# Two quarter-loads of gate weights change queues at the start of a fused layernorm, SSM and SwiGLU kernel

## The chip, the cores and the metric

The kernel runs on 1 core of one Trainium2 chip. The time is the device time of one execution in microseconds (us). Before the change it is 179.15 us (median of 3 runs, 179.12 to 179.2). Times inside an execution are counted from the start of the profiled span, which is about 1.7 us shorter than the device time. PE is TensorE, ACT is ScalarE, DVE is VectorE, SP is SyncE. The mean granted TensorE clock is 1.0 unless said.

## The reference, cut to what matters

```python
xn = _layernorm(x, axis=-1)                    # x: 2048 x 512, bf16
return x + _A_ref(xn, ...) + _B_ref(xn, ...)   # A: a diagonal SSM, B: SwiGLU

def _B_ref(x, w_gate, w_up, w_down):           # w_gate: 512 x 1376
    g = _silu(x @ w_gate)
    u = x @ w_up
    return (g * u) @ w_down
```

The gate product contracts over 512 rows of `w_gate`. The kernel holds them as four K tiles (0 to 3) of 128 rows. A gate output is four matmuls, one for each K tile, accumulated in PSUM. The loads discussed here bring the first 896 of the 1376 columns of `w_gate` (7 output tiles of 128); a later load brings the rest.

## The kernel before

The kernel records tasks with their dependences. It then orders ACT's, DVE's and Pool's tasks with a list scheduler of its own that works on estimated times. PE's and SP's tasks keep the order in which they were recorded. Only the first 13 us concern the change. In them, x tiles 0 to 3 are loaded and normalised while PE runs fillers (warm-up matmuls on constants), and then PE does the first gate matmuls in quarters of 128 tokens. The head of the load order is:

```python
x_load(0)                                    # 128 KB each, on SP's queue
x_load(1)
act_q = [dma("ld_touch", tch[0:16, 0:1], wg_v[0:128:8, 0:1, 0:2], [("tch",)], 16 * 4, eng="act")]
act_q.append(wg_load("a0", 0, 2, eng="act", order=(act_q[-1],)))   # K tiles 0, 1: 448 KB
x_load(2)
act_q.append(wg_load("a1", 2, 3, eng="act", order=(act_q[-1],)))   # K tile 2: 224 KB
wg_load("a2", 3, 4)                                                # K tile 3: 224 KB, on SP's queue
x_load(3)
# ...
act_table(AF.Sqrt, (act_q[-1],))             # small activation: brings the Sqrt table load with it (2.22 to 3.51 us)
```

DVE works through a fixed chain of statistics. "b" is half a tile's statistics, "s" aggregates them and lets ACT take the square root, "r" is the reciprocal, and "n" normalises half a tile. The half of x tile 2 stands ahead of the reciprocal of tile 1:

```python
for op, a, h in (("r", 0, 0), ("n", 0, 0), ("b", 1, 0), ("b", 1, 1), ("s", 1, 0), ("b", 2, 0),
                 ("r", 1, 0), ("n", 1, 0), ("n", 1, 1), ...
```

PE uses the K tiles one after the other for the first quarter: 7 matmuls (one for each of 7 output tiles) of K tile 0, 7 of K tile 1, 7 of K tile 2, 7 of K tile 3. The first transposes of x tile 1 stand after the fourth matmul of K tile 2:

```python
place = {(0, 2, 4): (1, 0), (1, 0, 2): (1, 1), ...}   # (quarter, first K tile, n): (x tile, half)
for q in range(4):
    for k0, k1 in (((0, 1), (1, 2), (2, 3), (3, 4)), ((0, 1), (1, 2), (2, 4)), ...)[q]:
        for n, (i, bk) in enumerate(tiles):
            if (q, k0, n) in place:
                xt_tile_fine(*place[(q, k0, n)])
            # ... matmuls of K tiles k0 to k1, start=(kt == 0), stop=(kt == KT - 1)
```

So the 1st, 8th, 15th and 22nd gate matmuls are the first users of K tiles 0, 1, 2 and 3.

## Time and profile before

| what | before |
|---|---|
| device time | 179.15 us |
| PE busy, share of the span | 98% |
| K tile 2 landed, first use (15th gate matmul) | 6.17, 6.49 |
| K tile 3 landed, first use (22nd) | 6.76, 7.13 |
| x2 landed | 5.89 |
| first 512-wide gate matmul | 12.93 |

Each of these loads reports in 16 parts, seen in the trace as 16 increments of its semaphore; the "landed" figures are the 16th and last of them. Two lines of the page show what bounds the kernel: busy time of each engine with its share of the span, and the shares of the chain of waits that ended last.

```profile
PE 173.9 (98%) x927; PEld 83.9 (47%) x935; DVE 162.5 (92%) x284; ACT 87.8 (49%) x116; POOL 9.3 (5%) x22
...
PE 98%; issue 0%; DVE 0%
```

PE is almost never idle and the chain runs through PE alone, so a change counts only if it moves a PE instruction. The timeline of the kernel before shows the start. Its columns are start, duration, engine, line, operation, output and inputs, count, and in brackets the engine's idle time before it and what ended that. A "q" after an engine marks its sequencer issuing a DMA.

```profile
0.79 1.34 SPq L402 DMA_DIRECT2D x_sb<-in_A_x_dram  x3
...
1.22 0.97 ACTq L402 DMA_DIRECT2D wg<-in_B_w_gate_dram  x2
...
2.17 0.43 SPq L402 DMA_DIRECT2D wg<-in_B_w_gate_dram  x1
2.22 1.28 ACT L466 ACT_TABLE_LOAD   x1 [2.22 <-issue]
...
3.88 0.29 ACT L524 ACTIVATE sd<-mv,epst 128x1 f32<-128x1 f32 x1
...
5.71 1.17 PE L803 MATMUL pb<-xnT,wg 128*128 128x128 bf16 x18
...
5.92 0.43 DVE L512 BATCH_NORM_STATS2 st<-x_sb 128x6 f32<-128x256 bf16 x1 [0.26 <-DMA x_sb<-in_A_x_dram]
...
6.84 0.29 PE L582 MATMUL pb<-ident,xn_sb 128*128 128x128 bf16 x2
...
12.93 1.03 PE L759 MATMUL pb<-xnT,wg 128*128 128x512 bf16 x4
```

The first 18 gate matmuls run without a break. DVE waits 0.26 us for x2. That puts off the reciprocal of tile 1, and PE stands still for 0.14 us before the transposes at 6.84. The same trace tells how long each weight load took from issue to landing (last column, us); the lines are K tiles 0 and 1, K tile 2 and K tile 3.

```profile
wg<-in_B_w_gate_dram ACTq DMA_DIRECT2D x1, 448.0 KB, 4.0
wg<-in_B_w_gate_dram ACTq DMA_DIRECT2D x1, 224.0 KB, 4.5
wg<-in_B_w_gate_dram SPq DMA_DIRECT2D x1, 224.0 KB, 4.6
```

The two loads of 224 KB take about equally long, but SP's was issued 0.47 us later (2.17 against 1.70) and lands 0.59 us later. The tile on SP's queue is the one that PE uses last.

### The profile page before, as it was taken

The page shows a single profiled execution, that of the slowest core. Times are in us where ns is not written, and L with a number is a line of the kernel's source. Part 1 is how long each engine was busy: PE and PEld are TensorE (multiplying, and loading weights), DVE is VectorE, ACT ScalarE, POOL GpSimd, SP SyncE. Part 2 cuts the span into 40 slices and gives each one's busy share as a digit, 9 for nine tenths or more (in the row PEclk, how much of TensorE's full clock was granted, in tenths as well). Part 3 has the DMA queues.
Part 4 walks back from the last instruction along what each step waited for, and adds up shares of the span by engine and source line. Part 5 has one row for each costly group of instructions (what it writes and reads, how often), then busy time and mean ns, then how long its engine had stood idle before and what let it go on. Part 6 is the DMA issues. An engine that isn't in the chain of part 4 may idle for free.

```text
span 177.5 us, 2421 instructions
## 1 busy us (share of the span) xinstructions
PE 173.9 (98%) x927; PEld 83.9 (47%) x935; DVE 162.5 (92%) x284; ACT 87.8 (49%) x116; POOL 9.3 (5%) x22
## 2 busy tenths in 40 slices
PE   8999999999999999999999999999999999999994
PEld 2894444444444444444444444444444444444743
DVE  2865999899999999999999999999899999999933
ACT  4679979789999665034565560000965520000000
POOL 3022300040000000310000000000000000000000
PEclk9999999999999999999999999999999999999999
DMA  5992694664951000002700000002000000001022
GB/s 155 326 365 67 139 124 96 167 132 101 358 123 24 0 0 0 0 30 69 126 18 0 0 0 4 0 30 76 12 0 4 0 0 0 0 0 53 10 89 89
DMA packets 22966, 12.37 MB, mean 70 GB/s; under 512 B 15180, under 2 KB 22956, under 8 KB 22956
## 3 DMA queue, kind: packets, MB, share of 16 engines
q1 hardware_dynamic: 22508, 11.54, 25.0%
q10 hardware_dynamic: 448, 0.69, 1.2%
q8 instruction: 7, 0.11, 0.3%
q14 instruction: 3, 0.02, 0.0%
HBM read 6.46 MB, written 2.10 MB: 48 GB/s over the span
## 4 chain that ended last, share of the span: by engine, by line
PE 98%; issue 0%; DVE 0%
PE pb L759 36%; PE pb L959 21%; PE pb L876 16%; PE pb L972 15%; PE pb L803 4%; PE pb L477 3%; PE pb L839 2%; PE pb L849 1%; PE pb L582 1%; DVE x_sb L977 0%
## 5 line engine op out<-in xcount | busy, mean ns | idle before, releaser
L916 DVE TENSOR_TENSOR_SCAN rot<-sm,car,rot 128x512 bf16<-128x512 f32 x32 | 39.0, 1266 | 0.1
L959 PE MATMUL pb<-wd,hT 128*128 128x512 bf16 (+3 forms) x194 | 38.1, 355 | 0.2
L759 PE MATMUL pb<-xnT,wu 128*128 128x512 bf16 x160 | 37.3, 380 | 0.0
L759 PE MATMUL pb<-xnT,wg 128*128 128x512 bf16 x132 | 31.3, 380 | 0.0
L972 PE MATMUL pb<-W,hss 128*128 128x512 bf16 (+2 forms) x140 | 28.1, 355 | 0.2
L876 PE MATMUL pb<-xnT,BT 128*128 128x512 bf16 x128 | 28.1, 379 | 0.0
L959 PEld LDWEIGHTS pb<-wd,hT 128*128 128x128 bf16 (+1 forms) x198 | 18.5, 98 | 19.9
L759 PEld LDWEIGHTS pb<-xnT,wu 128*128 128x128 bf16 x160 | 15.6, 98 | 18.9 <-issue 0.2
L771 ACT ACTIVATE sg<-pb 128x1024 bf16<-128x1024 f32 x20 | 20.1, 1024 | 8.6 <-PE pb L759 7.7
L829 ACT ACTIVATE uf<-pb 128x1024 bf16<-128x1024 f32 x20 | 20.5, 1026 | 7.2 <-PE pb L759 5.9
L972 PEld LDWEIGHTS pb<-W,hss 128*128 128x128 bf16 x144 | 13.5, 98 | 14.3
L759 PEld LDWEIGHTS pb<-xnT,wg 128*128 128x128 bf16 x132 | 12.7, 98 | 15.7 <-ACT xn_sb L506 0.4
L876 PEld LDWEIGHTS pb<-xnT,BT 128*128 128x128 bf16 x128 | 12.5, 98 | 15.1
L883 ACT ACTIVATE u_sb<-pb 128x1024 bf16<-128x1024 f32 x16 | 16.2, 1017 | 5.4 <-PE pb L876 5.4
L977 DVE TENSOR_TENSOR x_sb<-pb,x_sb 128x512 bf16<-128x512 f32 (+2 forms) x18 | 11.0, 623 | 3.5 <-PE pb L972 3.5
L831 DVE TENSOR_TENSOR hT<-sg,uf 128x1024 bf16<-128x1024 bf16 x20 | 13.3, 680 | 0.0
L506 ACT ACTIVATE xn_sb<-x_sb,nmr,rstd 128x512 bf16<-128x512 bf16 x8 | 6.0, 804 | 9.2 <-DVE nmr L503 9.2
L858 ACT ACTIVATE sg<-pb 96x1024 bf16<-96x1024 f32 x2 | 2.0, 1013 | 17.1 <-PE pb L839 17.1
L482 DVE BATCH_NORM_STATS2 st<-x_sb 128x6 f32<-128x512 bf16 x12 | 7.4, 681 | 3.1 <-DMA x_sb<-in_A_x_dram 3.1
L907 DVE TENSOR_TENSOR rot<-rot,cosT 128x2048 bf16<-128x2048 bf16 x8 | 9.7, 1215 | 0.1
L907 DVE TENSOR_TENSOR rot<-rot,sin 128x2048 bf16<-128x2048 bf16 x8 | 9.7, 1216 | 0.0
L907 DVE TENSOR_TENSOR rot<-u_sb,cosT 128x2048 bf16<-128x2048 bf16 x8 | 9.7, 1216 | 0.0
(81 smaller groups left out, 144.3 us busy)
## 6 DMA issues: line engine op xcount, KB each, us to landing
out_dram<-x_sb SPq DMA_DIRECT2D x15, 128.0 KB, 1.7
x_sb<-in_A_x_dram SPq DMA_DIRECT2D x3, 512.0 KB, 6.9
wd<-in_B_w_down_dram SPq DMA_DIRECT2D x1, 1280.0 KB, 6.3
wu<-in_B_w_up_dram SPq DMA_DIRECT2D x1, 768.0 KB, 5.5
wu<-in_B_w_up_dram SPq DMA_DIRECT2D x1, 608.0 KB, 7.6
x_sb<-in_A_x_dram SPq DMA_DIRECT2D x4, 128.0 KB, 3.5
wg<-in_B_w_gate_dram SPq DMA_DIRECT2D x1, 480.0 KB, 6.4
wg<-in_B_w_gate_dram ACTq DMA_DIRECT2D x1, 448.0 KB, 4.0
```

Of the source, the lines that this page charges most:

```text
L482: return g.add("dve", lambda e, a=a: e.bn_stats(out=st[:, a, :], in_=x_sb[:, a, :]), reads=[("x", a)], writes=[("st", a)], name="bnst%d" % ...
L759: inst = e.matmul(pbank[0:fs, bk, :].rearrange("p (j t) -> p j t", j=4), lhsT=w[:, kt, i * 128:i * 128 + fs], rhs=xnT[:, c % 2, :, kt, :], ...
L771: g.add("act", lambda e: e.activation(out=sg[rows, sl, 0:n, :].rearrange("p a t -> p (a t)"), in_=pair_f32(rows, bk, 512 * n), func=AF.Sil ...
L829: g.add("act", lambda e: e.activation(out=uf[rows, ul, 0:n, :].rearrange("p a t -> p (a t)"), in_=pair_f32(rows, bk, 512 * n), func=AF.Ide ...
L831: g.add("dve", lambda e: e.tensor_tensor(out=hT[rows, hb, i0:i0 + n, :], in0=sg[rows, sl, 0:n, :], in1=uf[rows, ul, 0:n, :], op=ALU.mult), ...
L876: inst = e.matmul(pbank[:, bk, :].rearrange("p (j t) -> p j t", j=4), lhsT=BT[:, ri, kt, pt * 128:(pt + 1) * 128], rhs=xnT[:, c % 2, :, kt ...
L883: g.add("act", lambda e: e.activation(out=u_sb[:, us].rearrange("p r t -> p (r t)"), in_=pair_f32(slice(0, 128), b0), func=AF.Identity), r ...
L907: tt = lambda out, a, b, op, r, w, nm: g.add("dve", lambda e: e.tensor_tensor(out=out, in0=a, in1=b, op=op), reads=r, writes=w, name="%s_% ...
L916: g.add("dve", lambda e, A0=A0, A1=A1, k=k, ri=ri, pt=pt: e.tensor_tensor_scan(out=A1[:, k, ri, :], data0=rr[:, pt:pt + 1].to_broadcast([1 ...
L959: inst = e.matmul(pbank[:, bk, 0:nc_], lhsT=hT[0:fs, hb, i, lt * 128:(lt + 1) * 128], rhs=wd[0:fs, i, c0:c0 + nc_], start=(i == 0), stop=F ...
L972: inst = e.matmul(pbank[:, bk, 0:nc_], lhsT=hss[:, hb, pt, ri, lt * 128:(lt + 1) * 128], rhs=W12[:, ri, pt, c0:c0 + nc_], start=False, sto ...
L977: g.add("dve", lambda e, bk=bk, a=a, c0=c0, nc_=nc_: e.tensor_tensor(out=x_sb[:, a, c0:c0 + nc_], in0=pbank[:, bk, 0:nc_], in1=x_sb[:, a, ...
```

## The change

Intent, as the diff and its words show it: x2 should meet less traffic. K tile 2 goes to SP's queue behind x2; K tile 3 goes to ACT's queue, behind the Sqrt table load, which can so begin earlier.

```diff
         x_load(2)
-        act_q.append(wg_load("a1", 2, 3, eng="act", order=(act_q[-1],)))
-        wg_load("a2", 3, 4)
+        wg_load("a1", 2, 3)
         x_load(3)
 ...
         act_table(AF.Sqrt, (act_q[-1],))
+        wg_load("a2", 3, 4, eng="act", order=(g.tasks[-1],))
+        hold = {"a2": g.tasks[-1]}
 ...
-        hold = {}
 ...
             reserved.clear()
+            hold["sd0"].od.add(hold["a2"])
```

`order` and `od` are order in the instruction stream, not waits. The last line keeps the first square root behind the issue of K tile 3.

## The prediction

> **What bounds the kernel.** TensorE: 98% busy on the page, and the chain of waits is 98% PE, so only what moves PE matters. The change touches the first 8 us. The timeline there shows fillers (warm-up matmuls) until about 5.0 us, the first gate matmul at 5.71, then 112 gate matmuls 56 ns apart with transposes of x between them. PE pauses there only before transposes: 0.14 us before the first one of x tile 1 (a matmul at 6.65, the transpose at 6.845), 0.03 at 7.67, 0.12 at 9.58. The last two follow ScalarE's evacuations and will recur. The first comes from VectorE: half-tile statistics of x2 stand in its order before the reciprocal of tile 1, and VectorE idled 0.26 us (5.66 to 5.915) for the landing of x2 (5.89).
>
> **Why x2 is late.** Issued at 1.71, its packets run only from 4.25 to 5.44, though x1 before it on SyncE's queue was done at 3.67. ScalarE issued K tile 2 at 1.70, just ahead. My reading: [...] x2's waited until most of K tiles 0 to 2 had drained. [...] from 3.75 to 4.25 ScalarE's moves alone at about 385 KB/us[...].
>
> **What the change does.** K tile 2 (224 KB) goes behind x2 on SyncE (issued about 2.17); K tile 3 goes to ScalarE behind the Sqrt table load and its small activation. The table load starts at about 1.73, not 2.22: worth nothing, as the first square root (3.88) waits for statistics (3.85). I doubt that K tile 3 is really issued after the table load: at 20.91 ScalarE's sequencer is at a wait while four later-executed activations are already queued[...]. I expect the issue at 1.8 to 2.3 (70%), else 3.0 to 3.8. Either leaves the first square root alone within 0.1 us.
>
> Estimates from this trace: x2's packets start about 3.6 and land by 5.2 to 5.5. Then K tiles 2 and 3 share about 385 KB/us (448 KB, 1.2 us): landings 6.2 to 6.6 for K tile 2 (before 6.17, needed at 6.485) and 6.3 to 6.9 for K tile 3 (before 6.76, needed at 7.13).
>
> **On the path.** VectorE's 0.26 us wait goes, the reciprocal of tile 1 comes 0.2 us sooner, PE's 0.14 us gap closes. Everything after is gapless PE, so the shift stays: minus 0.14 us, less some chance that K tile 2 is late (up to plus 0.3). Expected 179.05 us (before 179.15), range 178.75 to 179.4: within 2% 0.985, faster 0.005, slower 0.01.
>
> **What would show it.** Right: no VectorE idle time for x2, first transpose of tile 1 near 6.71, K tile 2's matmuls contiguous, first plain gate matmul (12.93) near 12.79. Wrong: PE pausing near 6.5 or 7.1 for weights; x2 still landing near 5.9[...]; first square root later than 3.9, so that the first gate matmul slips past 5.71.
>
> **What would make it wrong.** K tile 2 landing after 6.5 (it takes the place of the 6.76 landing); the issue on ScalarE blocking the square root; the kernel's static scheduler reordering later ScalarE or VectorE work from changed estimates, some tenths either way.

The sum: 179.15 less the gap of 0.14 is 179.01, and the chance of a late K tile 2 (up to plus 0.3) takes it to 179.05. What the trace itself shows of x2's delay: from 3.75 to 4.25 us ACT's queue moves all but alone, and from 4.25 to 5.25 both queues move. That x2's packets waited for K tiles 0 to 2 was the reading of these times, not shown; the start near 3.6 was an estimate that rests on it.

## The result, and the profile after

The changed kernel takes 179.74 us (median of 6 runs, 179.59 to 180.06), and the kernel before on the same chips 179.14 (6 runs, 178.94 to 179.47). The ratio is 1.0033, 95% interval 1.002 to 1.0046. Ratios here are the mean time of one kernel's fast runs over that of the other's fast runs of the same rounds, so they are not quite the ratio of the quoted medians. The change is within 2% and it is slower, by about 0.6 us, outside the predicted range.

The shares of the chain of waits of the changed kernel:

```profile
PE 94%; DMA 3%; SPq 1%; issue 0%; DVE 0%
```

A DMA is now in the chain. The timeline of the changed kernel (the edit moves most line numbers in this stretch by one):

```profile
0.79 1.34 SPq L402 DMA_DIRECT2D x_sb<-in_A_x_dram  x3
...
1.23 0.45 ACTq L402 DMA_DIRECT2D wg<-in_B_w_gate_dram  x1
...
1.71 1.28 ACT L465 ACT_TABLE_LOAD   x1 [1.71 <-PEq L1076]
1.78 0.42 ACTq L402 DMA_DIRECT2D wg<-in_B_w_gate_dram  x1
...
2.18 0.43 SPq L402 DMA_DIRECT2D wg<-in_B_w_gate_dram  x1
...
3.78 0.29 ACT L523 ACTIVATE sd<-mv,epst 128x1 f32<-128x1 f32 x1 [0.48 <-DVE mv L521]
...
6.01 0.95 PE L802 MATMUL pb<-xnT,wg 128*128 128x128 bf16 x14 [0.33 <-DMA wg<-in_B_w_gate_dram]
...
6.34 0.43 DVE L511 BATCH_NORM_STATS2 st<-x_sb 128x6 f32<-128x256 bf16 x1 [0.48 <-DMA x_sb<-in_A_x_dram]
...
7.38 0.38 PE L802 MATMUL pb<-xnT,wg 128*128 128x128 bf16 x4 [0.41 <-DMA wg<-in_B_w_gate_dram]
...
7.60 0.28 PE L581 MATMUL pb<-ident,xn_sb 128*128 128x128 bf16 x2
...
13.75 0.59 PE L758 MATMUL pb<-xnT,wg 128*128 128x512 bf16 x2
```

The run of 18 matmuls is now 14 and 4. Between them PE waits for `wg`: K tile 2 landed at 7.24, and the 15th matmul starts at 7.38 instead of 6.49. The weight loads of the changed kernel from issue to landing, in the order K tiles 0 and 1, K tile 3, K tile 2:

```profile
wg<-in_B_w_gate_dram ACTq DMA_DIRECT2D x1, 448.0 KB, 4.7
wg<-in_B_w_gate_dram ACTq DMA_DIRECT2D x1, 224.0 KB, 4.9
wg<-in_B_w_gate_dram SPq DMA_DIRECT2D x1, 224.0 KB, 5.1
```

Two more things are to be seen. K tile 3 was issued at 1.78, in the table load and not behind it. And x2 is not earlier but later (6.31). Part of this execution's delay is its own accident: in the trace one of the 16 parts of most loads from x1 on comes 0.4 to 0.7 us behind the other 15 (K tiles 0 and 1: 15 parts by 5.29, the last at 5.96), which also held the first gate matmul to 6.01. One profile cannot say how much of that belongs to the change. The first 15 parts can be compared without this accident: those of K tile 2 were in at 6.77 to 6.82 in all three profiles of the changed kernel, and at 6.10 and 6.15 in the two of the kernel before.

From there on nothing happens to the difference. The first 512-wide gate matmul starts at 13.75 instead of 12.93, and in both executions the device time (180.06 and 179.25) is 166.3 us more than that. The same difference, 166.30 to 166.33, stands in 13 of the 17 profiles, so the start of that matmul tells the time; the four exceptions are named below. The static scheduler did reorder some DVE and ACT work after 14 us, and this constant shows that it costs nothing.

### The profile page after: what moved, and what is told of

It reads as the page before. It is cut to its first block, busy times and chain, and to the rows that moved or that the text cites. A ratio compares the mean times of both kernels' runs of the same rounds, so it can differ in the third digit from the quotient of the medians.

```text
span 178.3 us, 2422 instructions
## 1 busy us (share of the span) xinstructions
PE 173.8 (97%) x927; PEld 83.8 (47%) x935; DVE 163.0 (91%) x284; ACT 88.3 (49%) x116; POOL 9.2 (5%) x22
## 3 DMA queue, kind: packets, MB, share of 16 engines
HBM read 6.46 MB, written 2.10 MB: 48 GB/s over the span
## 4 chain that ended last, share of the span: by engine, by line
PE 94%; DMA 3%; SPq 1%; issue 0%; DVE 0%
PE pb L758 35%; PE pb L959 21%; PE pb L876 15%; PE pb L972 15%; PE pb L802 3%; DMA wg<-in_B_w_gate_dram 3%; PE pb L839 2%; PE pb L849 1%; SPq L402 1%; PE pb L581 1%; DVE x_sb L977 0%
## 5 line engine op out<-in xcount | busy, mean ns | idle before, releaser
L972 PEld LDWEIGHTS pb<-W,hss 128*128 128x128 bf16 x144 | 13.4, 98 | 14.3
L876 PEld LDWEIGHTS pb<-xnT,BT 128*128 128x128 bf16 x128 | 12.5, 98 | 15.1
L907 DVE TENSOR_TENSOR rot<-u_sb,sin 128x2048 bf16<-128x2048 bf16 x8 | 9.7, 1218 | 0.0
```

The source lines that it names most:

```text
L876: inst = e.matmul(pbank[:, bk, :].rearrange("p (j t) -> p j t", j=4), lhsT=BT[:, ri, kt, pt * 128:(pt + 1) * 128], rhs=xnT[:, c % 2, :, kt ...
L907: tt = lambda out, a, b, op, r, w, nm: g.add("dve", lambda e: e.tensor_tensor(out=out, in0=a, in1=b, op=op), reads=r, writes=w, name="%s_% ...
L972: inst = e.matmul(pbank[:, bk, 0:nc_], lhsT=hss[:, hb, pt, ri, lt * 128:(lt + 1) * 128], rhs=W12[:, ri, pt, c0:c0 + nc_], start=False, sto ...
```

## The experiments

Theory T1: the loss is the wait for K tile 2. It took the later place on SP's queue, and PE needs it first. Rival T2: the moved table load, or the order of ACT's instructions, costs the time. Beside these, a question: what holds x2 back, if not what the prediction said?

The kernel before took 179.46 us (median of 9). Kernels are compared only within the same rounds.

### The table load alone

K tile 2 stays on ACT and K tile 3 on SP, as before; the table load goes ahead of ACT's last weight load. Against the changed kernel:

```diff
-        wg_load("a1", 2, 3)
+        wg_load("a2", 3, 4)
 ...
-        wg_load("a2", 3, 4, eng="act", order=(g.tasks[-1],))
+        wg_load("a1", 2, 3, eng="act", order=(g.tasks[-1],))
```

> Edit: the queues keep K tile 2 on ScalarE and K tile 3 on SyncE as before the change; only the Sqrt table load is moved ahead of ScalarE's last weight load. Theory T1 (the loss comes from K tile 2, needed first at about 6.5 us, now being the fifth transfer in SyncE's queue instead of the second on ScalarE's): no loss, 179.0 to 179.3 us, K tile 2 lands 6.1 to 6.4, no pause of the gate matmuls longer than 0.1 us for weights. Rival T2 (the table load or the order of ScalarE's instructions costs the time): 179.6 to 179.8 us, like the change.[...]

Measured: 179.29 us (median of 5), ratio to before 0.9994 (0.9981 to 1.0006). K tile 2 landed at 6.05. The timeline has the unbroken 18 again:

```profile
5.73 1.17 PE L802 MATMUL pb<-xnT,wg 128*128 128x128 bf16 x18
```

T2 is out: with ACT's first 38 us in the order of the changed kernel, apart from which tile its last load carries, no time is lost. (The scheduler's later order of DVE and ACT is here that of the kernel before. It is no rival: the loss arises before 13 us, and the 166.3 us hold with either order.) My reading of the prediction would also have x2 land before 5.5 here, as it is issued ahead of ACT's last load. x2 landed at 5.45, but the bulk of its packets began at 4.2, no earlier than in the kernel before (4.4 and 4.2). That speaks against the reading. ("Bulk" is here and below the ninth of a load's 128 packets.)

### The tiles alone

The table load stays where it was before the change; the two tiles exchange queues. Against before:

```diff
-        act_q.append(wg_load("a1", 2, 3, eng="act", order=(act_q[-1],)))
-        wg_load("a2", 3, 4)
+        act_q.append(wg_load("a2", 3, 4, eng="act", order=(act_q[-1],)))
+        wg_load("a1", 2, 3)
```

> Edit: K tiles 2 and 3 exchange queues, and nothing else; the table load stays behind ScalarE's weight loads as before the change. T1: the whole loss, 179.5 to 179.9 us, with TensorE pausing 0.3 to 0.6 us before the 15th gate matmul for K tile 2. T2: none, 179.0 to 179.3.

Measured: 179.63 us (median of 5), ratio 1.0012 (0.9999 to 1.0024). K tile 2 landed at 6.88, and the wait is back:

```profile
5.74 0.94 PE L803 MATMUL pb<-xnT,wg 128*128 128x128 bf16 x14
...
7.01 0.38 PE L803 MATMUL pb<-xnT,wg 128*128 128x128 bf16 x4 [0.33 <-DMA wg<-in_B_w_gate_dram]
```

This is T1's picture, and DVE's whole order is that of the changed kernel. By time alone the interval just reaches 1; the position of the 15th matmul is what tells.

### The load really behind the table load

The changed kernel, with K tile 3's load waiting on the semaphore of the small activation:

```diff
-        wg_load("a2", 3, 4, eng="act", order=(g.tasks[-1],))
+        wg_load("a2", 3, 4, eng="act", after=(g.tasks[-1],))
```

> Edit: the changed kernel, with K tile 3's load made to wait (semaphore) for the end of the small activation behind the table load, so that it is issued at about 3.35 us, as the change's words say, instead of 1.78. If the early issue of K tile 3 is what lets it run beside K tile 2 and delay it: K tile 2 lands 5.9 to 6.3 and the loss shrinks, to 179.0 to 179.4 us, unless K tile 3 now lands after 7.1 (then a pause there of as much). If K tile 2 is late merely because it is last in SyncE's queue behind x0 to x2: the same as the change, 179.6 to 179.9, K tile 2 near 6.8. T2 gives the same as the change as well, or worse by a later square root.

Measured: 179.92 us (median of 5), ratio 1.0023 (1.001 to 1.0037). The issue moved to 3.33. K tile 2 landed at 6.50 instead of 6.8 to 7.2, so K tile 3 beside it on the other queue is likely part of its delay (one profile). But K tile 3 now landed at 7.38, behind its need at about 7.1, and PE waited for it there (22nd matmul at 7.43). The wait was moved, not removed. (The profile is of the fastest of the five runs, 179.51; what the others lost beyond it was not traced.) x2 landed at 5.99, and its last packet began at 5.29, before K tile 3's first at 5.46. So of ACT's queue only K tiles 0 and 1 moved beside it: the first sign that those two hold it.

### The changed kernel again

> The changed kernel once more, for a second profile. The first shows one of the 16 parts of most landings from x1 on 0.5 to 0.7 us behind the other 15 (K tiles 0 and 1: 5.29, then 5.96), and TensorE waiting for K tiles 0 and 1 as well. If that straggler belongs to the change, it is here again and the first gate matmul starts near 6.0. If it was an accident of that execution, the first gate matmul starts near 5.6 to 5.7, only the pause for K tile 2 is left, and the profiled time is nearer 179.6 than 180.06.

Measured: 179.72 us (median of 5), ratio 1.0019 (1.0005 to 1.0033). The straggler (late last part) of 0.67 us in K tiles 0 and 1 was an accident (here the 15th part came at 5.27 and the last at 5.38; first gate matmul at 5.67). K tile 2 landed at 6.89 and the 15th matmul started at 7.02.

### Both tiles on SyncE

Against before (the kernel before took 179.34 us, median of 11):

```diff
-        act_q.append(wg_load("a1", 2, 3, eng="act", order=(act_q[-1],)))
+        wg_load("a1", 2, 3)
         wg_load("a2", 3, 4)
```

> Edit: before, but K tiles 2 and 3 both on SyncE's queue behind x2, in that order, so that ScalarE carries only K tiles 0 and 1. If K tile 2 was late in the changed kernel because K tile 3 ran beside it on the other queue: K tile 2 now lands 6.2 to 6.5 (packets of it alone after K tiles 0 and 1 are through), no pause over 0.15 us before the 15th gate matmul, K tile 3 lands 6.7 to 6.9, 179.2 to 179.5 us. If it is its place behind x0 to x2 alone: K tile 2 again near 6.8, and the loss is there. x2 starts near 4.25 again, as in all six profiles so far, if K tiles 0 and 1 alone hold it; near 3.6 if a second load on ScalarE held it (my blind reading).

Measured: 179.18 us (median of 6), ratio 0.9992 (0.9977 to 1.0007). K tile 2 landed at 6.13 and K tile 3 at 6.75, both in time. So K tile 2 was in time behind x2 on SP's queue when K tile 3 followed it there instead of running beside it (6.13, against 6.79 to 7.24 in the changed kernel). x2's bulk began at 4.14. The first 512-wide matmul was the earliest of all profiles (12.79), but this execution lost it later: PE waited before 25.25 for the transposed `B_im` (landed 25.20). SP issues that after x4 to x7 have landed (in the kernel before they landed at 15.44, and SP issued `B_re` at 15.52 and `B_im` at 19.66). The extra issue put their load from 6.62 to 7.10. Its landing came at 16.40 (15.44 before, and 14.3 to 16.2 in all 14 profiles in which the issue was not moved), so that the extra issue is the reason is likely, not shown.

### K tiles 0 and 1 behind x2 in order of issue

Against the table-load run, K tiles 0 and 1 move behind the table load on ACT's stream:

```diff
-        act_q.append(wg_load("a0", 0, 2, eng="act", order=(act_q[-1],)))
 ...
+        wg_load("a0", 0, 2, eng="act", order=(g.tasks[-1],))
         wg_load("a1", 2, 3, eng="act", order=(g.tasks[-1],))
```

> Edit: K tile 2 on ScalarE, K tile 3 on SyncE as in the run with the table load alone moved, but K tiles 0 and 1 are issued behind the table load too (about 1.30 instead of 1.23, or, if the table load holds up the issue, after x2's issue at 1.71). If [...] K tiles 0 and 1 hold x2 back: when they are issued after x2, x2's packets start before 3.3 and it lands before 4.8, while K tiles 0 and 1 land 5.3 to 5.8 (needed 5.7). If the issue moves by less than 0.1 us, nothing changes (179.1 to 179.5 us)  and x2's start stays near 4.25: then this run does not tell.

Measured: 187.7 us (median of 6), ratio 1.0469 (1.044 to 1.0498). It does not answer its question: the issue moved only to 1.29, still ahead of x2's at 1.71, and the bulk of x2's packets began at 4.37. The 8 us, which I had not expected, have nothing to do with the queues. With the changed estimates the kernel's own scheduler put the statistics of x4 to x7 between DVE's last two copies of transposed x, and x4 to x7 land after 16 us. Its timeline:

```profile
10.70 0.29 DVE L588 COPY xnT<-pb 128x256 bf16<-128x256 bf16 x1 [0.33 <-PE pb L581]
...
16.25 2.47 DVE L483 BATCH_NORM_STATS2 st<-x_sb 128x6 f32<-128x512 bf16 x4 [5.25 <-DMA x_sb<-in_A_x_dram]
...
18.91 0.26 DVE L588 COPY xnT<-pb 128x256 bf16<-128x256 bf16 x1
...
19.23 1.03 PE L802 MATMUL pb<-xnT,wg 128*128 128x128 bf16 x8 [7.00 <-DVE xnT L588]
```

PE stood still for 7 us, and the granted clock was 0.5 from 15.1 to 21.9 us (mean 0.981). It is the mishap that the prediction named for the changed kernel, at "some tenths" of a us; there it did not happen.

### K tile 3 used first

The changed kernel with its loads untouched, but in the first quarter PE uses K tile 3 before K tile 2:

```diff
-            place = {(0, 2, 4): (1, 0), ...
+            place = {(0, 3, 4): (1, 0), ...
-    for k0, k1 in (((0, 1), (1, 2), (2, 3), (3, 4)), ...
+    for k0, k1 in (((0, 1), (1, 2), (3, 4), (2, 3)), ...
-            start=(kt == 0), stop=(kt == KT - 1))
+            start=(kt == 0), stop=(kt == (2 if q == 0 else KT - 1)))
```

> Edit: the changed kernel, loads untouched, but TensorE uses K tile 3 before K tile 2 for the first x tile (the order in which they land). T1: the pause before the 15th gate matmul shrinks to under 0.15 us (K tile 3 lands 6.2 to 6.3), the 22nd then starts near 7.05 when K tile 2 is in (6.8 to 6.9), 179.2 to 179.5 us. If the loss came from anything else in the change: 179.6 to 179.9 as before.

Measured: 179.64 us (median of 6, 179.09 to 179.72), ratio 1.0009 (0.9991 to 1.0027): it cannot be told from before, and the median lies above what T1 expected. In the profile (179.41 us) the wait for weights is gone; x2 landed at 5.99, so the transposes of x tile 1 came at 6.94.

### The kernel before again

The kernel before, unchanged, for one look.

> The kernel before once more, for a second profile: K tile 2 lands 6.1 to 6.3, the first gate matmul at 5.6 to 5.8 and the first 512-wide one at 12.8 to 13.0; the size of the differences from the first profile is the noise against which landings of single profiles are read.

Measured: 179.43 us in one run (its state is unknown, as for every single run). The expectation was missed: here a straggler hit K tile 2 (15 parts by 6.15, the last at 6.70). The 15th matmul started at 6.83 and the first 512-wide one at 13.13. DVE's statistics of x2 have no wait here (no bracket):

```profile
5.57 0.37 DVE L512 BATCH_NORM_STATS2 st<-x_sb 128x6 f32<-128x256 bf16 x1
...
6.83 0.38 PE L803 MATMUL pb<-xnT,wg 128*128 128x128 bf16 x4 [0.26 <-DMA wg<-in_B_w_gate_dram]
```

So the kernel before can suffer the same wait, in one of its two profiles, by a straggler. The changed kernel waits in all three of its profiles, with one or without. How often stragglers come may be a reason why its ratios range from 1.0019 to 1.0033; the timed runs don't show it.

The kernel before took 179.31 us (median of 11).

### All gate weights on SyncE

```diff
-        act_q.append(wg_load("a0", 0, 2, eng="act", order=(act_q[-1],)))
         x_load(2)
-        act_q.append(wg_load("a1", 2, 3, eng="act", order=(act_q[-1],)))
+        wg_load("a0", 0, 2)
+        wg_load("a1", 2, 3)
         wg_load("a2", 3, 4)
```

> Edit: before, but all gate weights on SyncE's queue behind x2 in the order of need: x0, x1, x2, K tiles 0 and 1, K tile 2, K tile 3, x3; ScalarE carries only a 64-byte load. Question: what holds x2's first packets to about 4.1 to 4.4 us in all ten profiles so far, whatever ScalarE issued after K tiles 0 and 1? If K tiles 0 and 1 on ScalarE's queue do: x2's packets follow x1's without a hole, from 2.6 to 3.2, and x2 lands before 4.5. If x2 is late by itself (third load of the queue): it starts near 4.2 again. K tiles 0 and 1 then land 5.2 to 5.8 (needed 5.7), K tile 2 5.8 to 6.4, so the time is 179.0 to 179.6 us.

Measured: 179.42 us (median of 5), ratio 1.0002 (0.999 to 1.0014). x2's packets began at 2.9 and it landed at 4.06, 1.2 to 2.3 us earlier than in all profiles with K tiles 0 and 1 on ACT's queue (5.26 to 6.31). DVE does not wait for it (nor did it in the second profile of the kernel before; it is the start of the packets that tells). The timeline of this run has no bracket at x2's statistics:

```profile
5.57 0.38 DVE L512 BATCH_NORM_STATS2 st<-x_sb 128x6 f32<-128x256 bf16 x1
```

So K tiles 0 and 1 hold x2 back, not K tile 2. The time is no better: K tiles 0 and 1 now land at 5.70 and hold the first gate matmul to 5.83. And PE lost 0.11 us again near 25 us, where `B_im` landed at 25.06: the matmul at 25.11 starts 0.32 us after the one before it instead of 0.22.

### The changed kernel a third time

> The changed kernel a third time, on the same chip as the next two, as their yardstick: 179.5 to 180.0 us, K tile 2 lands 6.8 to 7.2, the 15th gate matmul about 0.13 us after that.

Measured: 179.71 us (median of 5), ratio 1.0021 (1.0009 to 1.0033). K tile 2 landed at 6.79, the 15th matmul started at 6.92, and the first 512-wide one at 13.29. This execution has no straggler of note (the last parts of x1 to x3 and of the K tiles come at most 0.06 us behind), and PE waits all the same:

```profile
6.92 0.38 PE L802 MATMUL pb<-xnT,wg 128*128 128x128 bf16 x4 [0.27 <-DMA wg<-in_B_w_gate_dram]
```

### K tile 2 one place further back

The changed kernel, with x3 ahead of K tile 2. The instruction order of PE, DVE, ACT and Pool is the same as in the changed kernel:

```diff
-        wg_load("a1", 2, 3)
         x_load(3)
+        wg_load("a1", 2, 3)
```

> Edit: the changed kernel with K tile 2 moved one place further back, behind x3 (128 KB) on SyncE's queue; the instruction order of all other engines is identical. T1, as a matter of dose: K tile 2 lands 0.3 us later than in the changed kernel of this call (7.1 to 7.3), and the time rises by as much, to 0.2 to 0.45 us above the changed kernel. If the landing of K tile 2 is not what costs the time: the same time as the changed kernel within 0.1 us.

Measured: 180.00 us (median of 5, 179.91 to 180.01), ratio to before 1.0035 (1.0023 to 1.0047); that is 0.29 us over the changed kernel (180.00 less 179.71; its runs, 179.61 to 179.83, don't reach these). K tile 2 landed at 7.18, 0.39 us later than there, and the first 512-wide matmul came at 13.69, 0.40 us later:

```profile
7.32 0.38 PE L802 MATMUL pb<-xnT,wg 128*128 128x128 bf16 x4 [0.69 <-DMA wg<-in_B_w_gate_dram]
```

This is the dose that T1 asked for. K tile 2 and x3 change places, nothing else is moved, and the time follows K tile 2's landing: 0.40 us between the two profiled executions (180.01 and 179.61), as between their 512-wide matmuls.

### K tile 3 used first, again

The same kernel as above.

> The changed kernel with TensorE using K tile 3 before K tile 2 for the first x tile, again, because the first measurement (ratio to before 1.0009, interval 0.9991 to 1.0027) could not tell; there the pause had moved to the first transpose of x tile 1, which waited for x2 (landed 5.99). T1: 0.15 to 0.4 us faster than the changed kernel of this call. If the loss is not the wait for K tile 2: no faster.

Measured: 179.60 us (median of 6), ratio to before 1.0007 (0.9991 to 1.0024). The expectation, 0.15 to 0.4 us under the changed kernel, was missed by the median (179.60 against 179.71); the means differ by 0.20 us, but half of the six times lie among or above those of the changed kernel. So time alone does not settle it. The six times fall apart: 179.15, 179.15, 179.47, 179.73, 179.80, 179.88. The profile is of the 179.73 run. Its first 18 gate matmuls are unbroken, but take 1.66 us where others take 1.17:

```profile
5.78 1.66 PE L802 MATMUL pb<-xnT,wg 128*128 128x128 bf16 x18
```

There the first ten start 0.107 us apart, up to 6.74, and from 6.82 on it is 0.056 us: only then did PE come to its full rate ("full clock" below). In the earlier profiles that came between 3.9 and 5.5 us, most often in the fillers. So the moment varies from execution to execution; what sets it is not shown. The delay here is 0.49 us (1.66 less 1.17). By my estimate it would in the changed kernel partly hide in the wait for K tile 2 (0.41 and 0.27 us in its first and third profiles).

The kernel before took 179.46 us (median of 11, 178.89 to 180.04).

### K tile 3 used first, two more profiles

The same kernel, one look each.

> The changed kernel with K tile 3 used before K tile 2, for a profile. So far its times fall in two groups, 179.1 and 179.7. In a profile of 179.73 TensorE's clock came to full only at 6.85 us[...]. T1 with this clock as the reason for the second group: a time under 179.3 has full clock before 5.6 and no pause for weights over 0.2 us; a time over 179.5 has full clock after 6 or another named landing (x2, K tiles 0 and 1) as the reason. If a run over 179.5 has full clock early and no such late landing, T1 lacks something.

> A second look at the same kernel as the run before, with the same expectation: under 179.3 us with full clock before 5.6 us, or over 179.5 us with full clock after 6 us or a late x2 or late K tiles 0 and 1 as the reason.

Measured: 179.37 and 179.36 us, between the two groups that I had named, so the expectation was missed. Full clock came at 5.23 and 3.56. The first profile shows no wait for weights, the second one of 0.08 us (K tile 3 landed at 6.32), and the transposes of x tile 1 follow at 6.87 and 6.89 in the two, held by DVE's wait for x2 (landed 5.92 and 5.94). The first 512-wide matmul starts at 13.04 and 13.05:

```profile
5.71 1.16 PE L802 MATMUL pb<-xnT,wg 128*128 128x128 bf16 x18
```

With the clock early, the three profiles of this kernel have that matmul at 13.04 to 13.10. The changed kernel has 13.29 to 13.75, and before 12.93 and 13.13. By these profiles, using the tiles in their order of landing takes most of the loss away. The timed runs, 1.0009 and 1.0007, neither show nor exclude that some of it stays. That the slow timed runs of this kernel were all late clocks is shown for one of them only.

### All on SyncE, K tiles 0 and 1 as two loads

Against the all-on-SyncE run (the matmuls' lists of what they wait for name the new load; not shown):

```diff
-        wg_load("a0", 0, 2)
+        wg_load("a0", 0, 1)
+        wg_load("a0b", 1, 2)
```

> A version that might beat both: all gate weights on SyncE's queue behind x2, as in the earlier run of that kind, and K tiles 0 and 1 as two loads, so that the first gate matmul needs 224 KB less (there it waited 0.13 us for both). x2 lands about 4.1, K tile 0 near 5.1, K tile 1 near 5.7 (needed 6.05), K tile 2 near 6.3 (needed 6.43), K tile 3 near 6.9 (needed 6.95). First 512-wide gate matmul at 12.7 to 12.85, so 179.0 to 179.2 us in executions without other delays: 0.1 to 0.3 us under before on the same chip.

Measured: 179.91 us (median of 6), ratio 1.0027 (1.0007 to 1.0047): slower, and the expectation was missed. x2 landed at 3.91 and K tiles 0 and 1 at 4.75 and 5.33, earlier than expected. But between 5 and 6 us the loads moved only 186 to 208 KB/us, where other kernels move 360 to 430, and K tile 2 landed at 6.94. Why the rate halved there is open. The clock in this profile also came late (6.46). And the three further issues on SP's queue push the later loads back (x4 to x7 issued at 8.04 instead of 6.62, landed at 16.86), and PE waited again, at 25.67:

```profile
25.67 1.69 PE L877 MATMUL pb<-xnT,BT 128*128 128x512 bf16 x7 [0.17 <-DMA BT<-in_A_B_im_dram]
```

No version was shown to beat the kernel before. The table load alone (0.9994), both tiles on SyncE (0.9992) and all on SyncE (1.0002) cannot be told from it. The both-on-SyncE, all-on-SyncE and split runs, and the one with the scheduler's mishap, are the four exceptions to the constant of 166.3 us.

## Why the prediction was wrong

- **The bound: right.** Only PE's position counts. What was lost before 13 us stayed to the end, with the constant of 166.3 us in both kernels.
- **The late issue: right.** K tile 3 was issued at 1.78 (forecast 1.8 to 2.3), not behind the table load of 1.28 us. ACT's sequencer ran ahead of its engine there: it issued the load 0.07 us after the table load's start (1.71) and 1.21 us before its end (2.99). How far ahead it can run no run shows.
- **The table load and the square root: right.** The table load started at 1.71 and was worth nothing; the first square root was at 3.78 to 3.91. The table-load run (0.9994) shows it.
- **"x2's packets start about 3.6 and land by 5.2 to 5.5": wrong, and this is the step that failed.** The prediction held that "x2's waited until most of K tiles 0 to 2 had drained", so taking K tile 2 out of the way would free x2. x2's bulk began at 4.1 to 4.4 in every profile with K tiles 0 and 1 on ACT's queue, whether K tile 2, K tile 3 or nothing followed them there. It began at 2.9 only when those two left the queue. The change does not move them. x2 landed at 6.31, 5.95 and 5.62 in the changed kernel, and at 5.89 and 5.42 before. The prediction had named "x2 still landing near 5.9" as what would show it wrong.
- **"landings 6.2 to 6.6 for K tile 2": the term of the sum that was mis-sized.** It was built on the early x2. K tile 2 landed at 7.24, 6.89 and 6.79 in the changed kernel, where it had been 6.17 and 6.70. PE is ready for it at about 6.5 (6.46 to 6.51 in four profiles where neither it nor K tiles 0 and 1 were waited for). In the six profiles in which the 15th matmul waits for K tile 2, apart from the split version's, it follows the landing by 0.13 to 0.14 us (there by 0.05). The prediction named this ("it takes the place of the 6.76 landing") as a risk of "up to plus 0.3"; it was the rule, and the 512-wide gate matmuls start 0.2 to 0.8 us later (13.29 to 13.75 against 12.93 to 13.13; the 0.8 includes the stragglers of the first profile).
- **"PE's 0.14 us gap closes": true but empty.** The transposes of tile 1 no longer wait, because PE reaches them later. There was little to win from the start: the gap came from x2's one late part in the single profile that the prediction read, and in the second profile of the kernel before DVE does not wait for x2.
- **The scheduler's reordering:** present and harmless here, but 8 us in one experiment.

The swap alone, its undoing and the dose show that the late K tile 2 is the loss; the changed order of use agrees in its profiles, though its times are too scattered to add proof. What stays open is why 448 KB on one queue hold back a load of the other queue for over a microsecond (x2's bulk at 4.1 to 4.4 with them, at 2.9 without), and whether the order of issue decides it. The run meant to tell that did not move the issue far enough (1.29, still ahead of x2's 1.71). Open too are the cause of the single late part among the 16, and the halved rate in the split version.

## What to carry to other kernels

Order loads by when their first user runs, over all queues together: list for each load its landing and its first use, and give the later place to the one that is used last. Here two equal loads changed places and the one needed 0.6 us earlier got the later landing (6.79 to 7.24, where it had been 6.17 and 6.70). Before crediting a change with freeing a transfer, find which transfer in front of it is the holder, by removing one at a time; and where a scheduler orders instructions from estimates, compare the order of every engine before believing a time.

## What else the traces show

- x2 waited behind an earlier load of the other queue: issued at 1.71, its bulk began at 4.1 to 4.4 with 448 KB issued on ACT's queue at 1.23, and at 2.9 without. In the kernel before, from 3.75 to 4.25, ACT's queue moved all but alone (together 403 KB/us; one packet of x2, at 4.10) while x2 had long been issued.
- Spreading the loads over two issuing engines did not change the total here (all on SyncE 1.0002), but which of two equal loads lands first followed their places in the queues (K tile 2 landed at 6.17 on ACT's queue and at 6.88 on SP's in the tiles-only run). SyncE's issue time was 0.43 us for one load of 224 KB. In the three kernels with further issues on SP's queue the landing of x4 to x7 came at 16.40 to 16.86 and PE waited near 25 us; in the 13 profiles of the constant it did not.
- The table load took 1283 ns. In the kernel before the next activation started 12 ns after its end, both times (3.519 and 11.590); the other 16 profiles show the same. A DMA was issued during a table load, 0.07 us after its start (1.78 and 1.71, changed kernel).
- There are single executions in which the last of a load's 16 parts comes 0.5 to 0.7 us after the 15th (5.29 and 5.96; 6.15 and 6.70).
- Full clock came between 3.56 and 5.53 us in 15 profiles with fillers from 0.8 us on, at 6.46 in one and at about 6.8 in another.
